# Float32 attention heads on one core: the softmax maximum is subtracted in PSUM and the exponential is taken after the transpose

## The chip, the cores and the metric

The kernel runs on one core of a Trainium2 chip. The metric is the time of one execution on the device in microseconds; the median of three runs of the kernel before the change is 1156.47 us (1153.44 to 1157.18).

## The reference

Attention over 8 batches of 8 heads (576 positions, 64 values per head) with a causal mask and a bias from a running sum, followed by a gated feed-forward layer (4608 tokens, 512 to 1536 to 512):

```python
scores = (1/np.sqrt(D)) * np.matmul(q, k.transpose(0, 1, 3, 2))
cum = np.cumsum(np.maximum(s, 0.0), axis=-1)
bias = -(cum[:, :, :, None] - cum[:, :, None, :])
scores = np.where(causal, -1e9, scores + np.minimum(bias, 0.0))
scores = scores - np.max(scores, axis=-1, keepdims=True)
attn = np.exp(scores)
attn = attn / (np.sum(attn, axis=-1, keepdims=True) + 1e-09)
attn_out = np.matmul(attn, v)
x = attn_out.transpose(0, 2, 1, 3).reshape(B * S, H * D)
out = (1 / (1 + np.exp(-(x @ w_gate))) * (x @ w_val)) @ w_out
```

## The kernel before

There are 64 heads. The first eight (batch 0, `NN = H`) are computed in float32 by functions whose names begin with `n_`; the other 56 work on pairs of float16 parts, and the feed-forward layer (`ffn_in` L648, `ffn_out` L676) does so too. A head's 576 queries are cut into five tiles t = 0 to 4, and tile t sees w = 64 + 128 t keys. Tiles are worked from 4 down to 0, one to a tick of the main loop (L741), so the float32 heads fill the first 40 ticks. While they run, the kernel also unpacks the weights from 64-bit words and splits them into float16 parts (`decode_weight` and `split_weight`, 18 steps): that is work for ACT and DVE, and each step needs one sum across partitions on POOL (L289, tile `wtot`).

A tile of a float32 head passes through these steps, each on another engine:

- POOL masks the 128 diagonal columns of the head's bias row `cr` (`mask_part`, L461, an affine select). The row was spread over the partitions by POOL as well (`spread_crow`, L409).
- PE multiplies queries with keys into PSUM (`n_s`, L575, tile `s`).
- DVE adds the bias, writes the negated logits into `e`, and finds their minimum `em` (`n_max`, L584; tile 4 takes two pieces).
- ACT takes the exponential of `e` in place, with `em` as the bias (L587).
- PE transposes `e` in blocks of 128 x 128, three blocks to a PSUM tile `nt_ps` (`n_turn`, L596), and ACT copies each PSUM tile into `p` (L597).
- PE multiplies `p` with the values `v` (`n_av`, L605); DVE divides by the sum (L611 to L615).

`e` lies in two buffers, one for tiles 0 to 2 and one for tiles 3 and 4. Each tile is padded at its right by 64 columns, which are set to zero once (L86), so that whole blocks can be transposed. The later heads use the same buffers and count on zeros there (`p_part`, L476).

A scheduler puts each engine's instructions into a fixed order when the kernel is built; on the chip every engine works through its list in that order. The float32 heads are emitted with high priority. On POOL, one list holds the masks, the spreading of bias rows, the sums across partitions (`wtot`, `vst`, `qkt`), memsets, and the issue of some loads of `v` (L161).

POOL's instructions belong to code libraries, and the build puts a reload ahead of an instruction whose library may not be in place. In the built program of before there is one such reload, of library 1, at L94, ahead of the first sum across partitions. In the built lists, of before and of the change, masks, memsets and DMA issues stand behind either library without a reload.

Of the kernel before, what the change touches and what calls it, by code (L numbers as in the profile page):

```python
# [8 lines left out]
F32 = mybir.dt.float32  # L9
# [3 lines left out]
AF = mybir.ActivationFunctionType  # L13
ALU = mybir.AluOpType
ADD_REDUCE = bass.bass_isa.ReduceOp.add

P = 128
GT = 256
PSCALE = 2.0 ** 14
MASKED = 1.0e30  # L20
# [3 lines left out]
def tile_attention_then_gated_ffn(  # L24
# [11 lines left out]
    nc = tc.nc  # L36
# [10 lines left out]
    TILES = [(0, 64, 64)] + [(64 + 128 * i, 128, 192 + 128 * i) for i in range(4)]  # L47
    NTL = len(TILES)


    SETS = (((0, 1, 2), (0, 1, 3), 6), ((3, 4), (0, 4), 9))
    PAD = NTL * P - S
    NN = H
# [4 lines left out]
    wp = ctx.enter_context(tc.tile_pool(name="wp", bufs=2))  # L58
# [15 lines left out]
    e_s = [cp.tile([P, n * P], F32, name=f"e_{i}") for i, (_, _, n) in enumerate(SETS)]  # L74
# [4 lines left out]
    e_t, pf_t = {}, {}  # L79
# [3 lines left out]
            e_t[t] = e_s[i][:, cols]  # L83
            pf_t[t] = p_s[i].rearrange("p l n -> p (l n)").bitcast(F32)[:, cols]
    for t, (q0, m, w) in enumerate(TILES):
        nc.gpsimd.memset(e_t[t][:, w:], 0.0)  # L86
    ident = cp.tile([P, P], F32, name="ident")
    scrap = wp.tile([P, 2, NTL * P], F16, tag="x16", name="scrap", bufs=1).bitcast(F32)
    count, junk = scrap[:, 0, :P], scrap[:, 1, :P]
# [9 lines left out]
    for g in range(0, P, 32):  # L99
        nc.vector.tensor_scalar(ident[g : g + 32, g : g + 32], count[g : g + 32, :32], count[g : g + 32, 32:33], None,  # L100
                                ALU.is_equal)
    nc.gpsimd.memset(e_t[0][64:, :], 0.0)
    expo = cp.tile([P, 2], F32, name="expo")
    nc.gpsimd.memset(expo[:, 0:1], 460.75)
    nc.gpsimd.memset(expo[:, 1:2], 204.75)
# [13 lines left out]
    def first(now=True):  # L119
        return tc.high_priority(1000) if now else ExitStack()  # L120
# [355 lines left out]
    def p_part(i, h_):  # L476

        nc.scalar.activation(p_s[h_][:, 0], e_s[h_], AF.Copy, scale=PSCALE)  # L478
        ts, first_block, n = SETS[h_]
        flat = p_s[h_].rearrange("p l n -> p (l n)")  # L480
        for t, kb in zip(ts, first_block):
            if t:
                nc.vector.scalar_tensor_tensor(flat[:, LOW[t] * P : (LOW[t] + t) * P], e_t[t][:, : t * P], PSCALE,  # L483
                                               flat[:, kb * P : (kb + t) * P], ALU.mult, ALU.subtract)
        tails = [t + kb for t, kb in zip(ts, first_block)]
        e_ = e_s[h_].rearrange("p (b g n) -> p b g n", g=2, n=64)
        p_ = flat[:, : n * P].rearrange("p (b g n) -> p b g n", g=2, n=64)
        for bs in (tails[:2], tails[2:]):
            if bs:
                b = slice(bs[0], bs[-1] + 1, max(bs[-1] - bs[0], 1))  # L490
                nc.vector.scalar_tensor_tensor(p_[:, b, 1], e_[:, b, 0], PSCALE, p_[:, b, 0], ALU.mult, ALU.subtract)
        PT[i, h_] = wp.tile([P, 2 * n, P], F16, tag=f"pt{h_}", name=f"pt{h_}_{i}")
        m = n + sum(ts)
        nc.sync.dma_start_transpose(PT[i, h_][:, :m], flat[:, : m * P])
# [35 lines left out]
                                    x16.rearrange("p l n -> p (l n)"))  # L530


    qT, kT, nS, nA = {}, {}, {}, {}

    def n_load(p):
        b, h0 = divmod(2 * p, H)
# [39 lines left out]
            nS[i, t].append((ps, a, b_))  # L576

    def n_max(i, t):
        q0, m, w = TILES[t]
        init = MASKED  # L580
        r = rl[i]
        for n, (ps, a, b_) in enumerate(nS.pop((i, t))):
            acc = wp.tile([P, 1], F32, tag=f"em{n}", name=f"em{i}_{t}_{n}", bufs=3)
            nc.vector.tensor_tensor_reduce(e_t[t][:m, a:b_], ps[:m, : b_ - a], r[:m, a:b_], -1.0, init,  # L584
                                           ALU.add, ALU.min, acc[:m])
            init = acc[:m]
        nc.scalar.activation(e_t[t][:m, :w], e_t[t][:m, :w], AF.Exp, bias=init, scale=-1.0)  # L587

    def n_turn(i, t):

        h_, groups = {4: (1, (6,)), 3: (1, (3, 0)), 2: (0, (3,)), 1: (0, ()), 0: (0, (0,))}[t]
        o = p_s[h_].rearrange("p l n -> p (l n)").bitcast(F32)
        for a in groups:
            ps = pp.tile([P, 512], F32, tag="gv", name=f"nt_ps_{i}_{t}_{a}")
            for kb in range(3):
                nc.tensor.transpose(ps[:, kb * P : (kb + 1) * P], e_s[h_][:, (a + kb) * P : (a + kb + 1) * P], ident)  # L596
            nc.scalar.copy(o[:, a * P : (a + 3) * P], ps[:, : 3 * P])  # L597

    def n_av(i, t):
        p, j = divmod(i, 2)  # L600
# [140 lines left out]
    for n in range(nticks + 12):  # L741
        if n == NTL * EARLY:
            more_room()
        i, t = divmod(n, NTL)
# [10 lines left out]
        if 2 <= n < nticks + 2:  # L755
            a, z = divmod(n - 2, NTL)
            if a < NN:
                with first():
                    n_turn(a, NTL - 1 - z)
            elif z in (1, 4):  # L760
                p_part(a, 1 if z == 1 else 0)
        if 1 <= n < nticks + 1:
            a, z = divmod(n - 1, NTL)
            if a < NN:
                with first():
                    mask_part(a, NTL - 1 - z)
                    n_max(a, NTL - 1 - z)
            else:
                mask_part(a, NTL - 1 - z)
                max_part(a, NTL - 1 - z)  # L770
        if 3 <= n < 3 + NTL * NN:
            with first():
                a, z = divmod(n - 3, NTL)
# [113 lines left out]
        if n >= NE and state["u"] < 2 * NF:  # L887
            fdone = min(NF, int((n - NE + 1) * FPT))
            while state["u"] < 2 * fdone:
                f = state["u"]  # L890
# [17 lines left out]
        m = n - (11 if n > 2 * NTL * H + 30 else 7)  # L908
        b = m // (NTL * H) if m >= 0 else 0
        if b >= 1:  # L910
            r = m - b * NTL * H + 1
# [39 lines left out]
```

## Time and profile before

| what | us |
|---|---|
| median of three runs | 1156.47 |
| span of the profiled execution (first to last instruction) | 1146.4 |
| difference between them: what lies around the span | 10.1 |
| busy in the span: PE / DVE / ACT / POOL | 1091.6 / 776.1 / 749.5 / 261.3 |
| first transposing instruction of the float32 heads starts (L596) | 12.2 |
| last copy of the float32 heads starts (L597) | 118.0 |

The profiler gives the span of one execution and not the time around it, so the profiled execution's own time is taken as its span plus the 10.1 us that the median run has beyond it. PE is busy for 95% of the whole span, but the page's 40 slices show the digits 6, 7, 8 and 7 for its first four, which is where the float32 heads lie. A busy share of the whole span says nothing about this stretch, which has to be read by itself.

### The profile page before, as it was taken

How to read it: one execution, taken by the hardware profiler on the slowest of the kernel's cores; microseconds unless marked ns; L12 is line 12 of the kernel's file. 1: busy time of each engine (PE TensorE's matmuls, PEld its weight loads, DVE VectorE, ACT ScalarE, POOL GpSimd, SP SyncE). 2: the span in 40 equal slices, each digit the busy share in tenths (PEclk: the TensorE clock that was granted, in tenths of full speed). 3: DMA queues.
4: the chain of work that ended last, by engine and by line, in shares of the span. 5: the costliest groups of instructions: out<-in, count | busy, mean ns of one | idle time of the engine just before them, and what ended most of it. 6: DMA issues, size and time to landing. Idle time of an engine off the chain costs nothing.

```text
span 1146.4 us, 30336 instructions
## 1 busy us (share of the span) xinstructions
PE 1091.6 (95%) x11644; PEld 853.5 (74%) x11644; DVE 776.1 (68%) x2395; ACT 749.5 (65%) x1465; POOL 261.3 (23%) x568
## 2 busy tenths in 40 slices
PE   6787888989999999999999999999999999999998
PEld 4566676658767887788777777778877887787775
DVE  6899999866787777776565677777777775222222
ACT  6989778667777777676665577767776764233222
POOL 6634233222232222121211122212222221000000
PEclk9889899999999999999999999999999999999999
DMA  9676868995989888777646498868887774000000
GB/s 280 201 217 161 185 139 181 183 189 130 171 164 175 164 178 167 141 150 138 145 79 139 89 178 166 166 144 171 156 161 138 150 124 88 13 20 20 1 19 19
DMA packets 445518, 157.62 MB, mean 137 GB/s; under 512 B 403583, under 2 KB 435839, under 8 KB 445374
## 3 DMA queue, kind: packets, MB, share of 16 engines
q1 hardware_dynamic: 418686, 127.38, 57.6%
q10 hardware_dynamic: 23328, 17.04, 4.9%
q0 software_dynamic: 3360, 11.27, 3.0%
q8 instruction: 91, 1.49, 0.5%
q14 instruction: 53, 0.43, 0.1%
HBM read 56.92 MB, written 9.58 MB: 58 GB/s over the span
## 4 chain that ended last, share of the span: by engine, by line
PE 76%; DMA 7%; DVE 5%; issue 5%; ACT 5%; SPq 1%; POOL 1%; ACTq 0%; DVEq 0%; POOLq 0%
PE gv L657 42%; PE o L687 22%; PE s L447 3%; PE s L446 3%; DMA qk<-in_q_dram 1%; PE av L506 1%; PE av L508 1%; PE av L507 1%; DMA v<-in_v_dram 1%; DVE e L471 1%; PE s L575 1%; DMA pt<-p 1%; DMA T<-T 1%; PE na_ps L605 1%; DMA nqk<-in_q_dram 1%
## 5 line engine op out<-in xcount | busy, mean ns | idle before, releaser
L657 PE MATMUL gv<-x,w 128*128 128x256 f16 (+3 forms) x6912 | 613.2, 246 | 5.3 <-DVE t2f L664 2.7
L657 PEld LDWEIGHTS <-w 128*128 128x128 f16 x6912 | 533.8, 98 | 61.5 <-issue 5.2
L687 PE MATMUL o<-w2all,h 128*128 128x512 f16 x1296 | 314.8, 379 | 0.0
L461 POOL TENSOR_SCALAR_AFFINE_SELECT rl<-rl 128x64 f32<-128x64 f32 (+1 forms) x280 | 111.5, 399 | 519.7 <-DVE em L471 465.3
L474 ACT ACTIVATE e<-e,em 128x576 f32<-128x576 f32 x280 | 154.6, 554 | 92.3 <-DVE em L471 90.2
L687 PEld LDWEIGHTS <-h 128*128 128x128 f16 x1296 | 123.6, 98 | 108.7 <-issue 2.4
L662 ACT ACTIVATE th<-gv,scb 128x256 f32<-128x256 f32 (+3 forms) x288 | 111.4, 412 | 139.3 <-PE gv L657 138.4
L664 DVE SCALAR_TENSOR_TENSOR t<-th,gv 128x256 f32<-128x256 f32 x192 | 80.2, 417 | 133.5 <-ACT th L662 132.5
L471 DVE CUSTOM_DVE_ANT_0 e<-s,rl,qkcf 128x288 f32<-128x288 f32 x280 | 135.8, 485 | 30.5 <-PE s L447 24.9
L672 ACT ACTIVATE h<-t,hsc 128x256 f16<-128x256 f32 x192 | 96.6, 503 | 80.0 <-DVE t L664 80.0
L483 DVE SCALAR_TENSOR_TENSOR p<-e,p 128x384 f16<-128x384 f32 x224 | 102.0, 495 | 40.2 <-ACT p L478 39.4
L673 DVE SCALAR_TENSOR_TENSOR h<-t,hsc,h 128x256 f16<-128x256 f32 x192 | 93.2, 486 | 43.3 <-ACT h L672 42.8
L478 ACT ACTIVATE p<-e 128x1152 f16<-128x1152 f32 x112 | 112.1, 1001 | 2.8
L506 PE MATMUL av<-v,pt 128*128 128x65 f16 x560 | 68.0, 193 | 6.9 <-DMA pt<-p 6.9
L507 PE MATMUL av<-v,pt 128*128 128x64 f16 x560 | 68.0, 192 | 0.0
L446 PE MATMUL s<-T 128*128 128x288 f16 (+2 forms) x246 | 64.6, 280 | 3.6 <-DMA T<-qk 2.6
L508 PE MATMUL av<-v,pt 128*128 128x65 f16 x560 | 67.9, 194 | 0.0
L447 PE MATMUL s<-T 128*128 128x288 f16 (+2 forms) x246 | 62.2, 282 | 2.4 <-DMA T<-T 2.4
L506 PEld LDWEIGHTS <-pt 128*128 128x128 f16 x560 | 52.4, 97 | 13.6 <-DMA pt<-p 8.8
L706 POOL DMA_DIRECT2D out_dram<-osb x34 | 19.4, 570 | 174.6 <-ACT osb L705 173.8
L409 POOL PARTITION_BROADCAST cr<-cr x63 | 57.5, 913 | 6.1 <-DVE em L584 5.7
L455 DVE TENSOR_SCALAR rl<-cr,qkcf 128x576 f32<-128x576 f32 x56 | 29.1, 520 | 40.1 <-POOL cr L409 39.9
(157 smaller groups left out, 1436.9 us busy)
## 6 DMA issues: line engine op xcount, KB each, us to landing
v<-v SPq DMA_DIRECT2D x56, 162.5 KB
out_dram<-osb POOLq DMA_DIRECT2D x34, 256.0 KB, 2.9
v<-in_v_dram SPq DMA_DIRECT2D x64, 128.0 KB
T<-T SPq DMA_DIRECT2D x82, 72.0 KB
t2f<-in_v_dram SPq DMA_DIRECT2D x20, 288.0 KB
qk<-in_q_dram SPq DMA_DIRECT2D x17, 288.0 KB
qk<-in_k_dram SPq DMA_DIRECT2D x17, 288.0 KB
w2all<-in_moe_w_gate_dram ACTq DMA_DIRECT2D x7, 512.0 KB
```

Of the source, the lines that this page charges most:

```text
L446: nc.tensor.matmul(ps[:, : b_ - a], lhs, T[i][:, 0, a:b_], start=True, stop=False)
L447: nc.tensor.matmul(ps[:, : b_ - a], lhs, T[i][:, 2, a:b_], start=False, stop=True)
L461: nc.gpsimd.affine_select(rl[i][:, q0:w], rl[i][:, q0:w], pattern=[[-1, m]], compare_op=ALU.is_ge, fill=-MASKED if i < NN else MASKED, bas ...
L471: nc.vector.tensor_tensor_reduce(e_t[t][:, a:b_], ps[:, : b_ - a], rl[i][:, a:b_], c, init, ALU.add, ALU.min, acc)
L474: nc.scalar.activation(e_t[t][:, :w], e_t[t][:, :w], AF.Exp, bias=init, scale=-1.0)
L478: nc.scalar.activation(p_s[h_][:, 0], e_s[h_], AF.Copy, scale=PSCALE)
L483: nc.vector.scalar_tensor_tensor(flat[:, LOW[t] * P : (LOW[t] + t) * P], e_t[t][:, : t * P], PSCALE, flat[:, kb * P : (kb + t) * P], ALU.m ...
L506: nc.tensor.matmul(AV[i][:, t], hi, v_[:, D : 2 * D + 1], start=kb == 0, stop=False)
L657: nc.tensor.matmul(ps[:, gv, a:e], w1[f][:, cc, gv, wl], x_of(b, cc)[:, xl, c0 + a : c0 + e], start=(c == 0), stop=(c == 3 * NC - 1))
L662: nc.scalar.activation(th[:, a:e], ps[:, 0, a:e], AF.Tanh, scale=scb[b][:, f : f + 1])
L672: nc.scalar.activation(h[:, 0], t2, AF.Copy, scale=hsc[:, f : f + 1])
L687: nc.tensor.matmul(ps[:m], h[:, hl, tt * P : tt * P + m], w2[f][:, wl], start=(f == 0 and c == 0), stop=(f == NF - 1 and c == 2))
```

## The change

The subtraction of the maximum moves from ACT to PE, and the exponential moves behind the transpose. DVE now keeps the logits with their own sign and finds the maximum. POOL negates the maximum of each tile into a column `nm`. PE transposes each block of logits into PSUM and then adds the negated maximum with a second transposing matmul, whose stationary operand is the column `nm` repeated 128 times. ACT takes the exponential while it reads PSUM, where it copied before. The padding columns hold -1e30 during the float32 heads, so that their exponential is zero, and are cleared to zero by five memsets behind the last float32 head.

```diff
     for t, (q0, m, w) in enumerate(TILES):
-        nc.gpsimd.memset(e_t[t][:, w:], 0.0)
+        nc.gpsimd.memset(e_t[t][:, w:], -MASKED)
...
-    nc.gpsimd.memset(e_t[0][64:, :], 0.0)
...
-    qT, kT, nS, nA = {}, {}, {}, {}
+    qT, kT, nS, nA, nmax = {}, {}, {}, {}, {}
+    tile_of = [[t for t, kb in zip(ts, first_block) for _ in range(t + 1)] for ts, first_block, _ in SETS]
+
+    def clear_pads():
+        for t, (q0, m, w) in enumerate(TILES):
+            nc.gpsimd.memset(e_t[t][:, w:], 0.0)
...
     def n_max(i, t):
-        q0, m, w = TILES[t]
-        init = MASKED
+        init = -MASKED
         r = rl[i]
         for n, (ps, a, b_) in enumerate(nS.pop((i, t))):
             acc = wp.tile([P, 1], F32, tag=f"em{n}", name=f"em{i}_{t}_{n}", bufs=3)
-            nc.vector.tensor_tensor_reduce(e_t[t][:m, a:b_], ps[:m, : b_ - a], r[:m, a:b_], -1.0, init,
-                                           ALU.add, ALU.min, acc[:m])
-            init = acc[:m]
-        nc.scalar.activation(e_t[t][:m, :w], e_t[t][:m, :w], AF.Exp, bias=init, scale=-1.0)
+            nc.vector.tensor_tensor_reduce(e_t[t][:, a:b_], ps[:, : b_ - a], r[:, a:b_], 1.0, init,
+                                           ALU.add, ALU.max, acc)
+            init = acc
+        nmax[t] = wp.tile([P, 1], F32, tag="nm", name=f"nm{i}_{t}", bufs=4)
+        nc.gpsimd.tensor_scalar(nmax[t], init, -1.0, None, ALU.mult)
...
             for kb in range(3):
-                nc.tensor.transpose(ps[:, kb * P : (kb + 1) * P], e_s[h_][:, (a + kb) * P : (a + kb + 1) * P], ident)
-            nc.scalar.copy(o[:, a * P : (a + 3) * P], ps[:, : 3 * P])
+                blk = ps[:, kb * P : (kb + 1) * P]
+                u = tile_of[h_][a + kb]
+                nc.tensor.matmul(blk, e_s[h_][:, (a + kb) * P : (a + kb + 1) * P], ident, start=True, stop=False,
+                                 is_transpose=True)
+                nc.tensor.matmul(blk, nmax[u].to_broadcast([P, P]), ident, start=False, stop=True, is_transpose=True)
+            nc.scalar.activation(o[:, a * P : (a + 3) * P], ps[:, : 3 * P], AF.Exp)
...
                     n_turn(a, NTL - 1 - z)
+                    if n == NTL * NN + 1:
+                        clear_pads()
```

The next two pieces show POOL's list from the end of the first head into the second. In this list `ISA` with a tile behind it is a sum across partitions (`wtot`) or the spreading of a bias row (`cr`), and a bare `ISA` is the reload of a library. Before:

```order
L461 AFFINE_SELECT cr_147<-cr_147 128x64
L289 ISA wtot_195<-wss_193 128x1
L161 DMA vsq_2_278<-in_v_dram 128x576
L289 ISA wtot_212<-wss_210 128x1
L409 ISA cr_186<-cr_186 128x576
L461 AFFINE_SELECT cr_186<-cr_186 128x128 x2
L161 DMA vsq_3_304<-in_v_dram 128x576
```

The same place after the change, where the lines of the kernel have moved (L591 is the negation, L460 the mask, L288 the sum, L408 the spreading):

```order
L460 AFFINE_SELECT cr_146<-cr_146 128x64
L288 ISA
L288 ISA wtot_194<-wss_192 128x1
L591 ISA
L591 TENSOR_SCALAR nm_0_331<-em_0_0_329 128x1
L160 DMA vsq_2_289<-in_v_dram 128x576
L288 ISA
L288 ISA wtot_211<-wss_209 128x1
L408 ISA cr_185<-cr_185 128x576
L460 AFFINE_SELECT cr_185<-cr_185 128x128
```

The negations stand between the masks, and the built program puts a reload of library 0 ahead of a negation that follows a sum or a spreading, and a reload of library 1 ahead of a sum or a spreading that follows a negation. In the whole list there are 39 reloads where there was one, and the 38 new ones all stand within the float32 heads: 19 ahead of negations, 11 ahead of `wtot`, 5 ahead of the spreading of a bias row, 2 ahead of `vst` and 1 ahead of `qkt`. The negations themselves are 40.

On PE, the place is the transposition of tiles 3 and 2 of the first head. Before:

```order
L596 MATMUL nt_ps_3_0_267<-ident,e_80 128x128 x3
L575 MATMUL s_4_288_309<-nk_157,nq_1_156 128x288
L575 MATMUL s_3_0_333<-nk_157,nq_1_156 128x448
L605 MATMUL na_ps_294<-v_0_149,p_1_82 128x65
L596 MATMUL nt_ps_2_3_283<-ident,e_79 128x128
```

After the change (L579 is the product of queries and keys, L602 the transpose, L604 the addition of `nm`, L613 the product with the values):

```order
L604 MATMUL nt_ps_3_0_274<-ident,nm_3_259 128x128
L579 MATMUL s_4_0_322<-nk_156,nq_1_155 128x288
L613 MATMUL na_ps_309<-v_0_148,p_1_82 128x65
L602 MATMUL nt_ps_2_3_294<-ident,e_79 128x128
L613 MATMUL na_ps_309<-v_0_148,p_1_82 128x65 x4
L604 MATMUL nt_ps_2_3_294<-ident,nm_2_287 128x128
```

Each of the 120 transposes has one matmul more behind it, which reads the column `nm` that POOL wrote for that tile. PE's list holds nothing that would let it pass over such a matmul while `nm` is not there.

## The prediction

> **What bounds the kernel now.** I read the stretches first, because the change touches the float32 heads only and these end at 118.3 us. The windows view gives busy time of each engine in that stretch, in the one behind it, and in the rest (columns: PE, PE's weight loads, DVE, ACT, POOL, granted clock, DMA share, GB/s).
>
> ```profile
> 0.00:118.30 118.30, 90.16 (x516) 70.24 (x517) 98.44 (x247) 100.54 (x191) 58.96 (x110) 0.88 0.75 210
> 118.30:260.00 141.70, 123.97 (x1218) 93.65 (x1218) 120.12 (x378) 106.63 (x198) 42.77 (x81) 0.98 0.87 176
> 260.00:1146.40 886.40, 877.47 (x9914) 689.65 (x9912) 557.57 (x1771) 542.36 (x1078) 159.56 (x377) 1.00 0.62 122
> ```
>
> Behind 260 us PE is busy for 877 of 886 us, and the change touches nothing there. So what the change gains or loses in the first 118.3 us shifts the end by as much, unless the stretch from 118.3 to 260 us gives some back. In the first stretch ACT (100.5) and DVE (98.4) are nearly full, PE has 28 us free, and POOL is idle for half of it: 118.3 - 59.0 = 59.3 us. The chain of waits, asked for 0 to 170 us, shows how ACT holds the path early on, with the exponentials and the weight steps in turn, and then DVE:
>
> ```profile
> 27.15 0.78 ACT e L587
> 27.92 1.06 ACT wa L272
> 28.98 0.56 ACT e L587
> ...
> 58.83 1.54 PE nt_ps L596 x6
> ...
> 76.19 1.14 DVE w2all L275
> ```
>
> **What the change removes.** The groups of lines within this stretch give ACT's exponentials and what follows them:
>
> ```profile
> L587 ACT ACTIVATE e<-e,em 128x576 f32<-128x576 f32 (+4 forms) x40 | 22.1, 563 | 2.0 <-DVE em L584 1.9
> L597 ACT COPY p<-nt_ps 128x384 f32<-128x384 f32 x40 | 18.4, 476 | 1.8 <-PE nt_ps L596 1.5 <-issue 0.3
> L596 PE MATMUL nt_ps<-ident,e 128*128 128x128 f32 x120 | 25.4, 304 | 2.8 <-ACT e L587 1.9 <-ACT p L597 0.7
> ```
>
> The 40 exponentials over `e` go: 22.1 us of ACT. The 40 copies become exponentials of the same 128 x 384 elements out of PSUM. No row shows that form; the copy has 476 ns, and the exponential of 128 x 448 in the L587 group has 672 ns by its form, so it costs between 0 and 0.2 us more each, 0 to 8 us in all. I take 0, since the copy has the very shape and source. The DVE reduction changes its sign and its operation and in tile 0 its partitions, not its elements per partition: no cost.
>
> **What it adds on PE.** There are 120 matmuls more of the form of L596. Six of these took 1.54 us in the chain above, at a granted clock of 0.57 in that part: (1.54 - 0.48) / 5 = 0.21 us from one to the next, with 0.48 the longest single one. At full clock three take 0.49 us where one is 0.28: 0.11 us each.
>
> ```profile
> L596 PE MATMUL nt_ps<-ident,e x120: 272/275/476, 12.2 to 117.0; 128*128 128x128 f32 x120
> 96.35 0.50 PE L596 MATMUL nt_ps<-ident,e 128*128 128x128 f32 x3
> 99.93 0.49 PE L596 MATMUL nt_ps<-ident,e 128*128 128x128 f32 x3
> 50.00:60.00 10.00, 6.11 (x29) 4.76 (x30) 8.00 (x13) 9.88 (x21) 3.48 (x5) 0.57 0.16 45
> ```
>
> So PE gets 13 to 25 us more, against 28 us free. If nothing else moved, this would about eat what ACT gains.
>
> **What it adds on POOL.** This is the term that decides. POOL gets 40 negations of 128 x 1 and five memsets for one, and the built list carries 38 reloads of a code library that were not there. The rows for POOL:
>
> ```profile
> L936 POOL MEMSET const-float32-0.0<- 128x1 f32 x1 | 0.1, 99 | 0.2 <-issue 0.2
> L418 POOL MEMSET v<- 128x10 f32 x4 | 0.6, 139 | 0.1
> L461 POOL TENSOR_SCALAR_AFFINE_SELECT cr<-cr 128x128 f32<-128x128 f32 (+1 forms) x40 | 30.3, 763 | 17.5 <-DVE em L584 13.7 <-DMA ws<-in_moe_w_gate_dram 1.5 <-DVE invw L131 0.9
> POOL cr L409 <- DVE em L584: 5.7, 1, 5.7
> L94 POOLq MODIFY_POOL_CONFIG  x2: 5/5/5, 2.2 to 2.2; - x2
> L94 POOL PARTITION_ALL_REDUCE scrap<-scrap x1: 394/394/394, 2.3 to 2.3; - x1
> ```
>
> A negation lies between the 0.10 us of the smallest memset and the 0.76 us of a mask; I take the 0.14 us of the 128 x 10 memset, 40 x 0.14 = 5.6 us, with 0.4 us for four memsets.
>
> The price of a reload is the unknown. The last two rows show the only one before: two instructions of 5 ns at 2.2 us, and the sum across partitions starts at 2.3 us. By that row a reload costs 0.1 us. But this program ends with library 1 in place and asks at L94 for library 1, so in any execution behind another it may have asked for what was there. The new reloads alternate between library 0 and library 1, so each of them changes the library. If the code then has to be fetched from memory, the nearest rows are fetches from DRAM that POOL issues itself, 288 KB each, and the longest fetch on the chain; the nearest load of tables on an engine is ACT's:
>
> ```profile
> L161 POOL DMA_DIRECT2D vsq<-in_v_dram x8: 562/582/719, 8.6 to 48.0; - x8
> ...
> DMA to landing us min/median/max: 3.3/6.0/6.8
> 118.38 7.38 DMA qk<-in_q_dram
> L562 ACT ACT_TABLE_LOAD x1 | 1.3, 1283 | 0.7 <-PEq L936 0.7
> ```
>
> So a reload has 0.1 us at the one end and 7.4 us at the other, with 1.3, 3.3 and 6.0 us between. I take 6.0 us, the median of POOL's own fetches: an estimate, since the library's size is in no row. 38 x 6.0 = 228 us.
>
> The Trainium skill, in the page "GPSIMD Engine Reference", section 2.1 (Instruction dispatch), says that the first call into a freshly loaded library pays for a load of code of about 6 us (5.95 us measured there) which no instruction in a profile shows. By it the 38 reloads would be 226 us, and the time 1348 us. The trace does not bear it out so far: at L94 the first call came 0.1 us after the reload, and no run here shows a change from one library to another.
>
> **The sum.** POOL in this stretch: 59.0 + 5.6 + 0.4 + 228 = 293 us. POOL's list is in order. Behind a negation that waits for DVE's maximum, or behind a reload, stand the next masks, the spreading of the next bias row, the sums `wtot`, memsets and the issue of `vsq`. DVE waits for the masks, PE for `nm`, ACT for PE, and the weight steps wait behind ACT's exponentials and for `wtot`. So all four engines go at POOL's pace, and the cover that hides these costs elsewhere is gone. POOL's waits do not all go: its waits for DVE's maximum, 13.7 + 5.7 = 19.4 us by the rows above, remain, as a negation cannot come ahead of its maximum; the others (59.3 - 19.4 = 39.9 us) become late arrivals of POOL itself. That makes 312 us for a stretch that took 118.3: 194 us more. From below, no wait remains and the 40 masks fall from 763 ns to the 295 ns that their median has when DVE is not beside them (40 x 0.47 = 18.7 us less): 274 us. From above, all 59.3 us of waiting remain: 352 us.
>
> ```profile
> L461 POOL TENSOR_SCALAR_AFFINE_SELECT rl<-rl x280: 240/295/2183, 104.9 to 963.3; 128x128 f32<-128x128 f32 x114, 128x64 f32<-128x64 f32 x26
> ```
>
> The gain on ACT and the cost on PE vanish in this: ACT has about 80 us of work in 312, and PE 115. The span becomes 1146.4 + 194 = 1340 us. The profiled execution's own time is its span and the 10.1 us that the median run (1156.47) has beyond it, so the sum stands against that median: **1350 us**. Of the stretch from 118.3 to 260 us I expect nothing back. In the order, the preparation of the first float16 head and five of the 18 weight steps stand behind the heads as before.
>
> **The rivals.**
> - **The main case with other prices.** With 3.3 us a reload POOL's stretch is 312 - 38 x 2.7 = 209 us and the time 1248 us; with 7.4 us it is 365 us and 1403 us. With the 38 us below and 40 us above from the waits the case reaches from about 1210 to 1440 us. Chance 0.64.
> - **A reload costs nothing (the other side).** The row L94 speaks for it: 0.1 us from reload to call, 38 x 0.1 = 4 us in all, which POOL's 59.3 idle us hide. Then the path is ACT's. If all 22.1 us of the exponentials lay on it, 1134 us; if all of PE's 25 us did instead, 1182 us. ACT holds the chain for parts of the stretch only, and PE's doubled transposes come onto it at 58.8 us (1.5 us more), so I put it at 1154 us. It decides against my forecast where a reload costs less than about 1 us: then POOL's sum is 59 + 6 + 38 + 19 = 122 us, about the length of the stretch now. It is also the case in which the reloads in the list do not do on the chip what the list says. Chance 0.14, of it 0.05 faster, 0.05 the same, 0.04 slower.
> - **A reload is like ACT's table load**, 1.28 us: 59 + 6 + 49 + 19 = 133 us with the fewest waits, 173 us with all of them, so 1171 to 1211 us; about 1185 us. Nothing speaks for a small fetch but that row. Chance 0.08.
> - **Two fetches to a reload.** The row L94 counts two instructions for one reload. Two fetches of 6.0 us one after the other give 228 us more, 1578 us; with half of the second hidden, 9.0 us a reload, 1464 us. Chance 0.14, most of it near the lower end.
>
> **How the numbers follow.** A measurement of this kernel can tell about 0.3% from no change, 3.5 us. The forecast is the likeliest case, 1350 us. The range of 1180 to 1470 us leaves out the free reload (0.14), the lower part of the table-load case (0.02) and the dear end of the double fetch (0.04). Slower: 0.64 + 0.08 + 0.14 + 0.04 = 0.90; the same 0.05; faster 0.05.
>
> **What would show it.** The profile after should have POOL's masks and negations spread to about 312 us, gaps on POOL ahead of the first instruction behind each reload, PE idle for `nm` in the transposes, a low granted clock there, and the stretch of PE at 99% starting about 194 us later but as long as before. If those gaps are near 0.1 us, the price is wrong and the time is near 1154 us; if POOL's gaps are long but the others have slack, the coupling is wrong.

## The result, and the profile after

The changed kernel takes 1370.24 us (median of 4 runs, 1366.60 to 1373.07), the kernel before 1155.05 us beside it: a ratio of 1.187, 95% interval 1.184 to 1.191. The forecast was 1350 us, with a range of 1180 to 1470 us.

The windows view of the changed kernel, cut where its last float32 copy-with-exponential ends, 141.8 us behind that, and at the end (columns as before: PE, PE's weight loads, DVE, ACT, POOL, granted clock, DMA share, GB/s):

```profile
0.00:340.20 340.20, 128.92 (x632) 107.39 (x632) 92.16 (x240) 82.28 (x146) 62.17 (x153) 0.62 0.25 70
340.20:482.00 141.80, 127.69 (x1229) 95.49 (x1229) 125.95 (x383) 108.71 (x202) 49.09 (x82) 0.99 0.89 174
482.00:1371.30 889.30, 877.58 (x9909) 690.44 (x9907) 557.76 (x1773) 542.68 (x1080) 159.73 (x377) 1.00 0.62 123
```

The stretch of the float32 heads grew from 118.3 to 340.2 us, by 221.9 us; the two behind it by 0.1 and 2.9 us. In the first stretch no engine is busy for more than 129 of 340 us. POOL, which sets the pace, is busy for 62 us, hardly more than before (59): by busy time it would be the last engine to suspect.

What POOL does instead is in its waits in this stretch (who waited for what: us in total, times, the longest). "Issue" is time in which the engine waited for nothing that the profile shows:

```profile
POOL nm L591 <- issue: 145.0, 19, 9.4
POOL wtot L288 <- issue: 60.3, 10, 6.2
POOL cr L408 <- issue: 29.7, 5, 6.0
POOL vst L172 <- issue: 13.7, 2, 7.7
POOL nm L591 <- DVE em L587: 8.1, 8, 3.4
POOL qkt L359 <- issue: 6.0, 1, 6.0
```

The unexplained gaps, 37 in number, stand ahead of instructions that the built list has a reload for, and sum to 145.0 + 60.3 + 29.7 + 13.7 + 6.0 = 254.7 us, 6.9 us each. The 21 negations without a reload ahead of them have no such gap. The 38th reload lies just behind this stretch, so that not all of them stand within the float32 heads: POOL idles for 6.9 us ahead of a sum at 351.1 us, which the view puts down to ACT, and the stretch that holds it grew by 0.1 us. A piece of POOL's timeline shows how they lie (start us, us, what, idle before it):

```profile
24.49 0.23 POOL L460 TENSOR_SCALAR_AFFINE_SELECT cr<-cr 128x64 f32<-128x64 f32 x1
30.95 0.40 POOL L288 PARTITION_ALL_REDUCE wtot<-wss  x1 [6.23 <-issue]
38.83 0.26 POOL L591 TENSOR_SCALAR nm<-em 128x1 f32<-128x1 f32 x1 [7.47 <-issue]
39.05 0.74 POOL L160 DMA_DIRECT2D vsq<-in_v_dram  x1
45.94 0.40 POOL L288 PARTITION_ALL_REDUCE wtot<-wss  x1 [6.15 <-issue]
```

These are the rows of the order piece shown with the change: a sum, a negation and a sum, each with its reload, 15 us from the one sum to the next where the kernel before took 3.8 us. A reload of library 1 costs about 6.1 us (109.7 us in 18 gaps), one of library 0 about 7.6 us (145.0 us in 19). The instruction that does it is in POOL's sequencer, with two records to a reload (38 records for 19 reloads at L591) of 6 to 123 ns each, so a list by duration does not show it:

```profile
L591 POOL TENSOR_SCALAR nm<-em x40: 197/260/1179, 18.8 to 338.0; 128x1 f32<-128x1 f32 x40
L591 POOLq MODIFY_POOL_CONFIG  x38: 6/77/123, 9.9 to 330.7; - x38
```

The other engines stand where the sum said they would, PE for the negated maximum, ACT for PE, and DVE for POOL's masks and sums (waits view, 0 to 340 us):

```profile
PE nt_ps L604 <- POOL nm L591: 160.8, 18, 21.7
ACT p L605 <- PE nt_ps L604: 154.3, 25, 26.4
...
DVE xe_w L124 <- POOL wtot L288: 97.3, 9, 14.4
DVE e L587 <- POOL cr L460: 87.7, 22, 12.9
```

The gaps lie on the path, too. The chain of work that ended last, asked for 0 to 345 us, is "issue" for 62.4% of that time, some 215 us; in the kernel before it is 13.1% of the first 118.3 us. The longest pieces are gaps of POOL: the last one shown here is the gap ahead of a negation that starts at 226.68 us (start us, us, what):

```profile
78.03 7.09 issue
...
162.89 8.78 issue
...
217.32 9.36 issue
```

### The profile page after: what moved, and what is told of

Its sections match the earlier page's. It is cut to its first block, busy times and chain, and to the rows that moved or that the text cites. A ratio compares the mean times of both kernels' runs of the same rounds, so it can differ in the third digit from the quotient of the medians.

```text
span 1371.3 us, 30657 instructions
## 1 busy us (share of the span) xinstructions
PE 1134.2 (83%) x11764; PEld 893.3 (65%) x11764; DVE 775.9 (57%) x2395; ACT 733.7 (54%) x1425; POOL 271.0 (20%) x612
## 4 chain that ended last, share of the span: by engine, by line
PE 65%; issue 18%; DMA 5%; DVE 5%; POOL 3%; ACT 2%; SPq 1%; ACTq 0%; POOLq 0%; DVEq 0%
PE gv L665 36%; PE o L695 17%; PE s L446 2%; PE s L445 2%; PE av L505 1%; PE av L507 1%; PE av L506 1%; PE nt_ps L604 1%; DMA qk<-in_k_dram 1%; POOL cr L460 1%; PE s L579 1%; DVE p L482 1%; POOL nm L591 1%; DVE e L470 1%; DMA pt<-p 1%
## 5 line engine op out<-in xcount | busy, mean ns | idle before, releaser
L460 POOL TENSOR_SCALAR_AFFINE_SELECT rl<-rl 128x64 f32<-128x64 f32 (+1 forms) x280 | 118.6, 424 | 511.2 <-DVE em L470 452.1
L604 PE MATMUL nt_ps<-ident,nm 128*128 128x128 f32 x120 | 44.8, 384 | 170.2 <-POOL nm L591 160.8
L604 PEld LDWEIGHTS nt_ps<-ident,nm 128*128 128x128 f32 x120 | 24.3, 203 | 177.2 <-POOL nm L591 176.4
L482 DVE SCALAR_TENSOR_TENSOR p<-e,p 128x384 f16<-128x384 f32 x224 | 103.1, 500 | 41.1 <-ACT p L477 40.5
L605 ACT ACTIVATE p<-nt_ps 128x384 f32<-128x384 f32 x40 | 19.5, 488 | 160.1 <-PE nt_ps L604 154.3
L587 DVE CUSTOM_DVE_ANT_0 e<-s,cr 128x288 f32<-128x288 f32 (+4 forms) x40 | 17.0, 429 | 98.1 <-POOL cr L460 81.1
L445 PE MATMUL s<-T 128*128 128x288 f16 (+2 forms) x246 | 64.4, 277 | 3.6 <-DVE em L470 3.5
L579 PE MATMUL s<-nk,nq 128*128 128x288 f32 (+4 forms) x96 | 43.8, 561 | 25.8 <-DVE em L587 25.2
```

The lines of the kernel that those rows point to most:

```text
L445: nc.tensor.matmul(ps[:, : b_ - a], lhs, T[i][:, 0, a:b_], start=True, stop=False)
L460: nc.gpsimd.affine_select(rl[i][:, q0:w], rl[i][:, q0:w], pattern=[[-1, m]], compare_op=ALU.is_ge, fill=-MASKED if i < NN else MASKED, bas ...
L604: nc.tensor.matmul(blk, nmax[u].to_broadcast([P, P]), ident, start=False, stop=True, is_transpose=True)
```

## The experiments

The trace names PE's wait for the negation first and longest. Three things had to be told apart: whether the reloads by themselves cost the time, whether PE's wait or POOL's list carries it to the end, and what the change is worth without them. Every ratio below is to the kernel before, timed beside it (1151.45 us in e1 to e4, 1151.37 us in e5 to e7, 1150.96 us in e8 and e9). The runs e4 to e8 start from e1: they have the negation on DVE by the line that e1 shows, and each shows only what it changes beyond that. The runs e3 and e9 start from the kernel before.

### e1 and e2: the negation on DVE, or on ACT

```diff
-        nc.gpsimd.tensor_scalar(nmax[t], init, -1.0, None, ALU.mult)
+        nc.vector.tensor_scalar(nmax[t], init, -1.0, None, ALU.mult)
```

> The changed kernel with one edit: DVE negates the maximum instead of POOL, so the 38 new reloads of POOL's library are gone from the built list. Theory A (the reloads in POOL's list are the whole loss): the loss of about 215 us goes, and what is left is the change as meant, 22 us less on ACT against 13 to 25 us more on PE and 40 small DVE instructions of about 0.1 us (4 us on a nearly full engine): 1145 to 1165 us, with the float32 heads ending at 110 to 125 us. Rival B (the loss comes from the longer chain itself, the added transposing matmuls at a low clock and the exponential out of PSUM): most of the loss stays, above 1250 us.

In e2 the line reads `nc.scalar.activation(nmax[t], init, AF.Copy, scale=-1.0)`.

> The changed kernel with the negation on ACT, again without the 38 reloads. Theory A: 40 instructions of about 0.2 us on ACT give back 8 of the 22 us that the exponentials took, so 1145 to 1170 us and not faster than with the negation on DVE by more than 5 us. Rival B: above 1250 us, as with DVE.

Measured: e1 1156.99 us, ratio 1.005 (1.003 to 1.007); e2 1161.20 us, ratio 1.008 (1.007 to 1.010). One word in one line takes back 213 us (some 210 us by the ratios, as the kernel before was 3.6 us slower beside the changed kernel than beside e1). Theory A holds and rival B falls. But the change as meant, without the reloads, is no gain either: e1 is slower than the kernel before by some 0.5%, 5.5 us.

### e3: the kernel before with unread negations on POOL

```diff
         nc.scalar.activation(e_t[t][:m, :w], e_t[t][:m, :w], AF.Exp, bias=init, scale=-1.0)
+        unread = wp.tile([P, 1], F32, tag="nm", name=f"nm{i}_{t}", bufs=4)
+        nc.gpsimd.tensor_scalar(unread[:m], init, -1.0, None, ALU.mult)
```

> The kernel before with 40 negations on POOL added whose results nobody reads; nothing else of the change. The built list has 34 new reloads (17 to each library). Theory A (POOL's list is in order, and a reload holds up the masks, sums and broadcasts behind it, whoever reads the negation): 17 reloads of about 7.6 us and 17 of about 6.1 us as the trace of the changed kernel has them, 233 us, on a POOL with 59 us idle, of which about 20 us remain as waits: 1335 to 1365 us. Rival C (the loss comes from PE and ACT waiting for the negated maximum, and the reloads by themselves fall into POOL's idle time): within 20 us of the kernel before, 1155 to 1175 us.

Measured: 1353.52 us, ratio 1.176 (1.174 to 1.178): 202 us more, and nobody reads the negations. So the wait of PE for the negated maximum, 160.8 us in the trace of the changed kernel, is where the loss is seen there, and it is not needed for the loss: the reloads in POOL's list are enough. Here the wait moves to others, DVE for the masks behind the reloads and PE for DVE (waits view of e3, 0 to 330 us):

```profile
DVE e L584 <- POOL cr L461: 97.1, 19, 13.3
DVE xe_w L125 <- POOL wtot L289: 83.3, 11, 13.3
...
PE s L575 <- DVE em L584: 128.4, 17, 17.0
```

Rival C falls. POOL's gaps are like those of the changed kernel: 126.3 us in 17 ahead of negations, and 64.0 + 37.9 + 8.7 = 110.6 us in 17 ahead of sums and spreadings.

```profile
POOL nm L589 <- issue: 126.3, 17, 10.0
POOL wtot L289 <- issue: 64.0, 10, 9.3
POOL cr L409 <- issue: 37.9, 6, 7.0
POOL vst L173 <- issue: 8.7, 1, 8.7
```

### e4: a smaller dose

```diff
         nc.vector.tensor_scalar(nmax[t], init, -1.0, None, ALU.mult)
+        if t == 2:
+            unread = wp.tile([P, 1], F32, tag="un", name=f"un{i}_{t}", bufs=2)
+            nc.gpsimd.tensor_scalar(unread, init, -1.0, None, ALU.mult)
```

> The negation on DVE, and one unread negation of a head's tile 2 on POOL: 8 of them, with 16 reloads in the built list (8 to each library), a dose of 16 instead of 38. Theory A: 8 x 7.6 + 8 x 6.1 = 110 us more on POOL; with all of its 59 us idle filled 1155 + 51 = 1206 us, with none filled 1265 us, about 1225 us. Rival D (a reload costs this much only where negations and sums alternate closely; single ones hide): 1155 to 1175 us. Rival C: the same, 1155 us.

Measured: 1234.63 us, ratio 1.073 (1.071 to 1.074), which is 77.6 us above e1 for 16 reloads, 4.9 us each. The whole dose gave (1370.24 - 1156.99) / 38 = 5.6 us each. Rivals C and D fall: single reloads do not hide. From 16 to 38 each further reload adds (1370.24 - 1234.63) / 22 = 6.2 us, close to the gap of 6.9 us. So the first ones are partly covered by POOL's idle time, as the bounds of the expectation had it.

### e5: the added matmuls left out

```diff
-                nc.tensor.matmul(blk, e_s[h_][:, (a + kb) * P : (a + kb + 1) * P], ident, start=True, stop=False,
+                nc.tensor.matmul(blk, e_s[h_][:, (a + kb) * P : (a + kb + 1) * P], ident, start=True, stop=True,
                                  is_transpose=True)
-                nc.tensor.matmul(blk, nmax[u].to_broadcast([P, P]), ident, start=False, stop=True, is_transpose=True)
```

> The negation on DVE, and the second transposing matmul left out (the maximum is not subtracted). It sizes the 120 added matmuls by themselves, against the same kernel with them (1157.0 us). If they are on the path (PE's 13 to 25 us more eat what ACT gains): 1132 to 1147 us. If they lie in PE's free time and DVE bounds the float32 heads: within 4 us of 1157.

Measured: 1159.16 us, ratio 1.007 (1.004 to 1.009), not below e1 (1.003 to 1.007). The 120 matmuls cost nothing that shows; by the two intervals they can be worth 3 us at most, where 13 to 25 us were in question. So they lie in PE's free time and are not what eats ACT's gain.

### e6: an execution that ends with library 0

```diff
             ffn_out(*units[u], tiles=(tt,), last=True)
+    unread = wp.tile([P, 1], F32, tag="un", name="un_end", bufs=1)
+    tc.keep_in_program_order(nc.gpsimd.tensor_scalar(unread, gmax, -1.0, None, ALU.mult))
```

> The negation on DVE, and one unread negation on POOL behind everything else, so that an execution ends with library 0 and the reload at its start changes the library, which before it did not. If a reload is free only where its library is in place: a gap of about 6 us now shows on POOL ahead of the first sum across partitions near the start, where before it was 0.1 us; up to 8 us at the end (the second reload, partly behind the last output) and up to 6 us at the start on top of 1157.0 us, 1160 to 1172 us. If a reload is free at the start of a program for another reason: the gap stays at 0.1 us, and the time within 9 us of 1157.

Measured: 1166.09 us, ratio 1.013 (1.010 to 1.016), 9.1 us above e1. The reload at L94 now has a gap behind it; here are its records in e6, then in the changed kernel, where it is as short as it was before:

```profile
L94 POOLq MODIFY_POOL_CONFIG  x2: 4/4/4, 6.4 to 6.4; - x2
L94 POOL PARTITION_ALL_REDUCE scrap<-scrap x1: 402/402/402, 15.6 to 15.6; - x1
```

```profile
L94 POOLq MODIFY_POOL_CONFIG  x2: 4/4/4, 6.3 to 6.3; - x2
L94 POOL PARTITION_ALL_REDUCE scrap<-scrap x1: 423/423/423, 6.4 to 6.4; - x1
```

From reload to first call it is 9.2 us in the one and 0.1 us in the other. The gap was expected at about 6 us and is longer than any ahead of a sum in the changed kernel (7.7 us), though e3 has one of 9.3 us; why is not shown. The reload at the end has a gap of 7.1 us, which ends at 1133.9 us, beside PE's last work. The same instruction is free or dear by what the execution before it left in place.

### e7: the same dose late in the program

In `max_part`, behind the exponential of the later heads:

```diff
+        if t == 2 and 24 <= i < 32:
+            unread = wp.tile([P, 1], F32, tag="un", name=f"un{i}", bufs=2)
+            nc.gpsimd.tensor_scalar(unread, init, -1.0, None, ALU.mult)
```

> The negation on DVE, and 8 unread negations on POOL in heads 24 to 31, with 16 reloads there, in the stretch where PE is busy for 99% and POOL for 18%. Theory A (a reload holds up only POOL's own list): 110 us of reloads go into POOL's idle time, and PE runs on, as its work there waits for POOL with some heads of lead: 1155 to 1170 us. Rival E (a reload also stops other engines or the DMA queues, or POOL's lead is short): up to 1157 + 110 = 1267 us.

Measured: 1214.76 us, ratio 1.055 (1.053 to 1.058), 57.8 us above e1: 3.6 us for each of the 16 reloads. Theory A fails. The time lies within what rival E allowed, which named two ways: that a reload stops other engines too, or that POOL's lead is short. The gaps of the 16 reloads lie between 359 and 527 us, and about half of their time is hidden and half is not. Here are the windows from 355 to 530 us of e1 and then of e7:

```profile
355.00:530.00 175.00, 174.34 (x2137) 139.34 (x2138) 133.76 (x435) 127.37 (x255) 40.53 (x95) 1.00 0.81 162
355.00:530.00 175.00, 137.99 (x1492) 106.91 (x1490) 90.11 (x298) 86.70 (x173) 30.95 (x77) 0.89 0.56 118
```

PE, which was idle for 0.7 us, is idle for 37.0 us, though POOL is busy for 40.5 of the 175 us in e1. A reload does not stop PE by itself: in the gap from 391.7 to 398.0 us PE is busy all the time. The waits of e7 from 355 to 530 us name the way:

```profile
DVE rl L454 <- POOL cr L408: 38.6, 7, 7.0
PE s L445 <- DVE em L470: 31.6, 11, 4.6
DVE e L470 <- POOL rl L460: 27.8, 10, 4.2
```

DVE waits for the spreading of the next head's bias row and for masks that stand behind a reload. PE's list has the products of queries and keys in a fixed place, and these wait for DVE; the feed-forward matmuls behind them cannot pass. So POOL's lead over PE is mostly shorter than one reload: behind gaps of 5.9 to 7.4 us PE still waits, for up to 4.6 us. Idle time of an engine says how much work fits, not how long a single delay may be.

PE's idle time is not the whole loss. Over the two profiled spans, 1209.9 us in e7 and 1158.2 us in e1, PE is idle for 31.7 us more and busy for 20.1 us more, with the same 11764 matmuls; the granted clock is 0.97 against 0.99, and 0.89 against 1.00 in the windows above.

### e8 and e9: why the change without reloads gains nothing

In e1 ACT is busy for 84 us of the stretch of the float32 heads, where it was 100.5 us, and still that stretch is 5.6 us longer, 123.9 us for 118.3:

```profile
0.00:123.90 123.90, 94.89 (x651) 79.77 (x652) 99.95 (x296) 84.24 (x155) 64.15 (x119) 0.93 0.75 208
```

Two waits stand out on ACT in e1 (waits view, 60 to 125 us):

```profile
ACT jq L356 <- issue: 5.5, 1, 5.5
ACT jq L356 <- DMA qk<-in_q_dram: 4.4, 1, 4.4
```

The second of these is the one that the experiment is about. The squares `jq` of the second float16 pair stand in ACT's list ahead of the last exponentials and wait for a load. They are held back:

```diff
-            pin(nc.scalar.activation(junk, t[:, i].rearrange("p h c d -> p (h c d)"), AF.Square,
-                                     accum_out=ss[:QP, i : i + 1]))
+            square = nc.scalar.activation(junk, t[:, i].rearrange("p h c d -> p (h c d)"), AF.Square,
+                                          accum_out=ss[:QP, i : i + 1])
+            if spare or p == NN // 2 + 1:
+                tc.keep_in_program_order(square)
```

> The negation on DVE, and the squares of the second float16 pair's queries and keys held behind the work written before them, so that ACT has the last exponentials of the float32 heads ahead of them and not behind. In the trace of the kernel with the negation on DVE, ACT waited 4.4 us for the load of those queries with exponentials behind it. Theory F (ACT's freed time is given back in such waits in its own order): 3 to 6 us less than 1157.0, so 1151 to 1154 us, about the kernel before. Rival G (DVE bounds the float32 heads with or without ACT's relief): within 2 us of 1157.

> The control: the same hold in the kernel before. There the squares came behind the last copies of the float32 heads in the trace already (125.8 us against 118.0 us), so both theories expect the kernel before within 4 us, 1148 to 1156 us. If it gains as much as the other, the hold is worth something by itself.

Measured: e8 1154.79 us, ratio 1.0035 (1.0018 to 1.0052); e9 1151.55 us, ratio 1.000 (0.998 to 1.002). The wait of 4.4 us is gone from ACT's list in e8, and the hold by itself is worth nothing (e9). But e8 is 2.2 us below e1, between what the two theories expected, and its interval overlaps that of e1 (1.0032 to 1.0067), so it does not settle whether this wait was what ate the gain.

The first wait, 5.5 us put down to issue, was left in place, and e8 still has 5.2 us of it. In e1 ACT issues two loads at that time, which take 4.63 and 1.86 us (the first two rows below); the same two lines took 0.55 to 0.86 us a load in the kernel before. The longest piece of the chain of e1 from 76 to 100 us falls there (the third row):

```profile
81.71 4.63 ACTq L252 DMA_DIRECT2D ws<-in_moe_w_out_dram  x1
86.38 1.86 ACTq L259 DMA_DIRECT2D ws<-in_moe_w_out_dram  x1
85.22 5.09 issue
```

That is about the 5.5 us by which e1 is slower than the kernel before, but no run takes this wait away, and e2, whose trace does not have it, is not faster. It is a candidate and not a shown cause. No version ran faster than the kernel before.

## Why the prediction was right, and where it was off

- **The term that decides, the reloads.** 38 reloads at 6.0 us were put at 228 us; 37 gaps in the stretch sum to 254.7 us, 6.9 us each. The mechanism was the one forecast; the term was mis-sized by 27 us, as the estimate did not tell the two libraries apart (6.1 and 7.6 us). That the price came so near is partly luck: it was the median of fetches of 288 KB that POOL issues, and no run shows how much a reload moves, or that it is like those.
- **The sum for the stretch.** 312 us was forecast, 340.2 us measured. Of the 28 us, 27 are the reloads. POOL's own work was put at 65 us and is 62.2; the waits were put at 19.4 us and are 340.2 - 62.2 - 254.7 = 23.3 us. That the waits agree is luck in part: they were to be waits for DVE's maximum, and of those the waits view has only 8.1 + 3.1 = 11.2 us. Inside POOL's work two errors cancel: the negations take 17.4 us where 5.6 were put, and the 40 masks fell from 30.3 to 17.2 us, which the sum had only in its lower bound. The 295 ns used there for a mask without DVE beside it are the median of 280 masks of later heads, and that row says nothing of what DVE does; the mean here is 430 ns:

```profile
L591 POOL TENSOR_SCALAR nm<-em 128x1 f32<-128x1 f32 x40 | 17.4, 435 | 153.3 <-issue 145.0 <-DVE em L587 8.1
L460 POOL TENSOR_SCALAR_AFFINE_SELECT cr<-cr 128x128 f32<-128x128 f32 (+1 forms) x40 | 17.2, 430 | 3.6 <-DVE em L587 3.1
```

- **The exponential out of PSUM.** It was put at the price of the copy. In e1 its median is 491 ns, and the copy's was 479 ns in the kernel before: under 1 us for all 40.
- **The row L94.** The prediction set the price of 0.1 us aside, because the program may have found its library in place. e6 shows that this was so.
- **From the span to the time.** Here the working was wrong. The span grew by 224.9 us, not 194, while the median grew by 215 us. The prediction took 10.1 us to lie around the span; the runs that give both numbers have about 2 us there (1373.07 us with a span of 1371.3). So the profile of before came from an execution of about 1148 us (1146.4 and 2), a fast one of its kind, and the other 8 us are the spread between executions. These 8 us, and 3 us by which the profiled execution of the changed kernel was above its median, offset part of the 31 us missing from the span; 20 us of the miss are left, 1350 for 1370.
- **The part behind the heads** was to give nothing back; it grew by 0.1 and 2.9 us.
- **The coupling.** "All four engines go at POOL's pace" holds, and e3 shows that it does not need the new dependence of PE on the negation. The masks and sums behind a reload are enough.
- **The rivals.** A free reload was put at 1154 us; e1, in which the reloads are gone, has 1157 us. The two that priced a reload at 1.28 us or at 9 to 12 us fall by the gaps. The remark that PE's added matmuls would about eat ACT's gain is wrong: e5 shows them hidden. What keeps ACT's 16 us (100.5 to 84.2) from shortening the stretch stays open. DVE is busy for 100 of the 123.9 us in e1, and loads and the 5.09 us beside ACT's issue of loads are on its chain, but none of them was shown to be the cause.

## What to carry to other kernels

Before an elementwise instruction is put on POOL because POOL is idle, look in the built list for reloads of its code library: here one word, `gpsimd` for `vector`, brought 38 of them and 213 us. Price an added stall by the list it stands in and by the lead that this list has, not by the engine's busy share. And where a trace names one long wait, try the cause without the instruction that waits, as e3 did: the wait moved and the time stayed.

## What the runs showed of the hardware that was not expected

- A change of POOL's library costs about 6.1 us to library 1 and 7.6 us to library 0 in the changed kernel (6.5 and 7.4 us in e3), up to 9 to 10 us in single cases (10.0 us to library 0 in e3, 9.3 us to library 1 in e3 and e6), and 0.1 us where the library is already in place, also across executions (e6). The profile mostly shows it as "issue" ahead of POOL's next instruction, with POOL not busy.
- Sixteen reloads in a stretch in which, without them, PE is full and POOL 77% idle still cost 57.8 us (e7): POOL's lead over DVE and PE is mostly shorter than one reload, and PE then runs at a lower granted clock (0.89 for 1.00).
